# Four edits to the attention half of a bucketed-attention and mixture-of-experts kernel: PSUM banks of the turned halves, order of the routing work, copies between partition halves, making of the first heads

## The chip, the cores and the metric

One core of a Trainium2 chip runs the whole kernel. The metric is the device time in microseconds (us), the median of several runs, lower is better. Engines are named as the profile names them: PE (TensorE), DVE (VectorE), ACT (ScalarE), POOL (GpSimd), SP (SyncE, which here only issues DMAs).

## The reference

Attention over 4 batches, 8 heads, 768 positions, head size 64, in which a query sees only the keys that fall into its own hash bucket (6 sign bits of a projection); its result is fed to a top-1 mixture of 8 experts.

```python
q_bits = (einsum('bhsd,dk->bhsk', q, proj) > 0); k_bits = (einsum('bhsd,dk->bhsk', k, proj) > 0)
mask = q_bucket[:, :, :, None] == k_bucket[:, :, None, :]
scores = np.where(mask, q @ k.T / np.sqrt(D), -1e9)
attn = softmax(scores)                        # with 1e-9 added to the sum
x = (attn @ v)                                # (3072 tokens, 512)
e_idx = argmax(x @ w_gate); gate_w = softmax(x @ w_gate)[e_idx]
eom = sigmoid(x @ w_output_gate)
out[t] = gate_w * eom[e_idx] * (relu(x @ w1[e_idx]) @ w2[e_idx])
```

## The kernel before

**Heads and steps.** Heads are taken in 16 pairs. A pair is 12 steps, a step is 128 queries of one head; 192 steps, in blocks of 6 (`PER`). Each step has two parts that run 6 steps apart (`LAG`): `scores(s)` (L539) makes 8 matmuls into a `ps_s` tile, two `float32r` terms of queries against two of keys (`qh`, `ql`, `kh`, `kl`: high and low parts) and one product of bucket bits (`bb`); DVE reads the tile back into `sc` with its row minimum (L542); `soft` (L550) is the exponential on ACT; `normal` (L557 to L560) makes reciprocals of the row sums on DVE and scales `sc` on POOL; `transposed` (L580) turns `sc` on PE, 12 transposes of 64x64 blocks into two PSUM tiles (first and second half), which ACT copies to `pts` (L586). Once a block, `weighted` (L597) multiplies `pts` with `v`.

**PSUM.** `ps_s` and `ps_t` have two buffers each, `ps_a` and `ps_m` one. The first turned half always goes to `ps_t`. The second goes to `ps_t` at k = 0 (k is the step's place in its block), to `ps_m` at odd k, to `ps_a` at even k (L572 to L575). `weighted` accumulates in `ps_a`; the projection to bits (`project`, L436), `logits` (L631), `tokens` (L641), `prefix` (L698) and `table` (L239) use `ps_m`.

**Making a head.** For each head, POOL makes `qh`, `kh` (L488, L489), DVE makes `ql`, `kl` (L494, L497). Rows 0 to 63 of a tile hold the first half of the positions, 64 to 127 the second; both partition halves must hold all queries, so SP copies the halves across: four copies of `qh`, `ql` (L501, L502) and six of the bits (L517). The first head is made apart (`first_head`).

**Routing.** After each batch the tokens' experts, gates and table entries are worked out in small pieces (`routing`) that are planned into the steps of the next batch: `block(step, when, fn)` puts a piece at a named place inside the first step of a block ("early", "amid", "logits", "matmuls", "behind"), `plan(step, fn)` at a step's end. The order on PE, DVE, ACT and POOL is the order in which the program is written (`MANUAL`); SP's order is chosen by the scheduler.

**Late part and experts.** From step 170 on (`late`), the busiest expert's first weights are loaded and split on POOL (`early_w1`, L180 and L183) while attention ends. After the last step come the experts (L325), in which PE has almost no idle time; the change leaves them as they are.

Of the kernel before, what the change touches and what calls it, by code (L numbers as in the profile page):

```python
# [20 lines left out]
NB = 6  # L21
P = 128
# [37 lines left out]
def lsh_attention_then_moe(  # L60
# [22 lines left out]
    nc.scalar.dma_start(pj, proj)  # L83
    thr, scl, set0 = (pj[:, D + i:D + i + 1] for i in range(3))
    pjc = cst.tile([P, 2, 32], F32, name="pjc")
    nc.vector.memset(pjc, 0.0)

    def signed():

        for h in range(2):  # L90
            hs = slice(h * D, (h + 1) * D)
            src = pj[hs, 32 * h:32 * h + NB]
            for m, sg in ((0, 1.0), (1, -1.0)):
                c = 2 * NB * h
                nc.gpsimd.tensor_scalar(pjc[hs, m, c:c + NB], src, sg, 0.0, ALU.mult, ALU.add)
                nc.gpsimd.tensor_scalar(pjc[hs, m, c + NB:c + 2 * NB], src, -sg, 0.0, ALU.mult, ALU.add)
# [124 lines left out]
    def table_rhs(pool, oa, oh, gt, tk, n):  # L221

        rhs = pool.tile([P, 3, n, E * NCH], F32, name="t_rhs")
        nc.vector.tensor_tensor(rhs[:, 2].rearrange("p n (e a) -> p n e a", e=E),
                                oh[:, :, :, None].broadcast_to([P, n, E, NCH]),
                                oa[:, :, None, :].broadcast_to([P, n, E, NCH]), ALU.mult)
        for i, val in ((0, tk), (1, gt)):
            nc.vector.tensor_tensor(rhs[:, i], rhs[:, 2], val[:, :, None].broadcast_to([P, n, E * NCH]), ALU.mult)
        return rhs
# [155 lines left out]
    with ExitStack() as actx:  # L385
# [11 lines left out]
        at, around = {}, {}  # L397

# [26 lines left out]

        def bits_of(g, j):
            return halves[(2 * g + j) % 4]
# [15 lines left out]
        def tiles(g, j):  # L443
            st = pairs[g]
            for k, n in (("qh", S), ("ql", S), ("kh", HS), ("kl", HS)):
                st.setdefault(k, [None, None])[j] = hp.tile([P, n], F32R, name=k)
            return (st[k][j] for k in ("qk", "qh", "ql", "kh", "kl"))

        def first_head():

            qk, qh, ql, kh, kl = tiles(0, 0)
            bb = bits_of(0, 0)
            first = slice(0, HS)
            pp = ps_m.tile([P, HS], F32, name="ps_m")
            for m in range(2):
# [3 lines left out]
            nc.scalar.activation(qh[:, first], qk[:, first], AF.Copy, scale=-0.125)  # L459
            nc.vector.tensor_tensor(kl, qk[:, KEYS], f32(kh), ALU.subtract)  # L460
            nc.vector.scalar_tensor_tensor(ql[:, first], qk[:, first], -0.125, f32(qh[:, first]),
                                           ALU.mult, ALU.subtract)
            bt = hp.tile([P, HS], F32R, name="bt", bufs=2)
            nc.vector.tensor_scalar(bt, pp, 0.0, set0, ALU.is_gt, ALU.is_equal)
            bt = f32(bt)
            for h in range(2):
# [4 lines left out]
            def query_bits(n, h):  # L471
                c = (n ^ h) * HS
                nc.scalar.activation(bb[h * D:h * D + 2 * NB, c:c + HS], bt[32 * n:32 * n + 2 * NB], AF.Copy, scale=PEN)

            query_bits(0, 0)
            query_bits(0, 1)
            nc.vector.scalar_tensor_tensor(ql[DOWN, KEYS], qk[UP, first], -0.125, f32(qh[UP, first]),
                                           ALU.mult, ALU.subtract)
            for x in (qh, ql):
                nc.sync.dma_start(f32(x)[UP, KEYS], f32(x)[DOWN, first])  # L480
            return query_bits

        def split_hi(g, j):
            qk, qh, ql, kh, kl = tiles(g, j)
            if g == 0:
                nc.scalar.activation(qh[:, 0:HS], qk[:, 0:HS], AF.Copy, scale=-0.125)
            else:
                nc.gpsimd.tensor_scalar(qh[:, 0:HS], qk[:, 0:HS], -0.125, 0.0, ALU.mult, ALU.add)  # L488
            nc.gpsimd.tensor_scalar(kh, qk[:, KEYS], 1.0, 0.0, ALU.mult, ALU.add)  # L489

        def split_lo(g, j, m):
            st = pairs[g]
            if m == 0:
                nc.vector.scalar_tensor_tensor(st["ql"][j][:, 0:HS], st["qk"][j][:, 0:HS], -0.125,  # L494
                                               f32(st["qh"][j][:, 0:HS]), ALU.mult, ALU.subtract)
            else:
                nc.vector.tensor_tensor(st["kl"][j], st["qk"][j][:, KEYS], f32(st["kh"][j]), ALU.subtract)  # L497

        def turn_over(x):
            x = f32(x)  # L500
            nc.sync.dma_start(x[DOWN, KEYS], x[UP, 0:HS])  # L501
            nc.sync.dma_start(x[UP, KEYS], x[DOWN, 0:HS])  # L502

        def spread_hi(g, j):
            turn_over(pairs[g]["qh"][j])

        def spread_lo(g, j):
            turn_over(pairs[g]["ql"][j])

        def spread_bits(g, j):  # L510
            bt, bb = f32(pairs[g]["bt"]), f32(bits_of(g, j))
            for m in range(2):
# [32 lines left out]
        def soft(s, sc, mn):  # L545
            if s % GROUP == 0:
                sums[s // GROUP] = sp.tile([P, GROUP], F32, name="rsum")
# [3 lines left out]
                                 accum_out=sums[s // GROUP][:, k:k + 1])  # L551
# [10 lines left out]
        def transposed(s, pr):  # L562
# [10 lines left out]
            else:  # L573
                second = (ps_t, "ps_t") if last or s % PER == 0 else (ps_m, "ps_m") if s % 2 else (ps_a, "ps_a")
# [10 lines left out]
            for h in range(2):  # L585
# [33 lines left out]
        def routing(b):  # L619
# [112 lines left out]
            def columns():  # L732
                st["rhs"] = table_rhs(gp, st["oa"], oh, gate[:, ts], toki[:, ts], NT)
# [22 lines left out]
        for g in range(NP):  # L756
            s0 = 12 * (g - 1)
            if g >= 2:
                if g > 2:
                    plan(max(s0 - 20, 9), lambda g=g: load(g, (0,)))  # L760
                    plan(max(s0 - 16, 10), lambda g=g: load(g, (1,)))
                    block(s0 - PER, "matmuls", lambda g=g: project(g))
                else:
                    plan(10, lambda g=g: project(g))
                for j in range(2):
                    block(s0 + PER * j, "head", lambda g=g, j=j: split_hi(g, j))
                    block(s0 + PER * j, "early", lambda g=g, j=j: split_lo(g, j, 0))
                    block(s0 + PER * j, "amid", lambda g=g, j=j: split_lo(g, j, 1))
                    block(s0 + PER * j, "behind", lambda g=g, j=j: spread(g, j))
            elif g == 1:  # L770
                plan(1, lambda: split_hi(1, 0), lambda: spread_hi(1, 0))
                plan(2, lambda: project(1), lambda: split_hi(1, 1), lambda: spread_hi(1, 1))
                plan(3, lambda: load(2, (0,)))
                for j in range(2):
                    plan(3, lambda j=j: spread_bits(1, j))
                    for m in range(2):
                        plan(4 + 2 * j + m, lambda j=j, m=m: split_lo(1, j, m))
                    plan(5 + 2 * j, lambda j=j: spread_lo(1, j))
                plan(5, lambda: load(2, (1,)))
                plan(6, lambda: load_v(0))  # L780
            if g >= 1:
# [469 lines left out]
```

## Time and profile before

| | |
|---|---|
| median of 3 runs | 784.33 us (783.89 to 787.59) |
| profiled execution, its own time | 785.98 us |
| its span, first to last instruction | 784.3 us |
| PE busy | 731.6 us, 93% |
| mean granted TensorE clock | 0.971 of full speed |
| attention, to 2 us after the last step's scores are read (L542) | 457.8 us |
| from there to the end | 326.5 us |

The profile is one execution. The span leaves out 1.7 us around it. Matmuls are pipelined, so a busy PE is not PE at its peak, but a stretch in which PE has idle time or a granted clock below 1 has time that PE itself did not need. A block is cut in the tables where its first `sc` instruction (L542) starts.

### The profile page before, as it was taken

The numbers are of one execution on the slowest core, as the hardware profiler recorded it, in microseconds if no ns is written. First come the engines' busy times: TensorE is split into PE (matmuls) and PEld (weight loads), VectorE is DVE, ScalarE is ACT, GpSimd is POOL, SyncE is SP. The second block draws the span as 40 slices with busy tenths as digits, with TensorE's granted clock in tenths as the row PEclk, the third lists the DMA queues.
The fourth block names the chain that finished last, engine by engine and source line by source line (L and its number), as shares of the span: only waits on it lengthen the run. The fifth ranks groups of instructions, "written<-read, shape, count | busy, mean of one in ns | idle before, by whom it ended". The sixth has DMA issues, their size and how long they took to land. (4 is left out here: it accounts for less than half of the span.)

```text
span 784.3 us, 17592 instructions
## 1 busy us (share of the span) xinstructions
PE 731.6 (93%) x6591; PEld 602.3 (77%) x6591; DVE 493.6 (63%) x1046; ACT 452.3 (58%) x927; POOL 372.5 (47%) x446
## 2 busy tenths in 40 slices
PE   6699999988998988999798899999999999999996
PEld 4568776666875676775586568988999999989894
DVE  7578777768776866776788668236262636364640
ACT  4579888857787775887786751244251524353330
POOL 4355655444354534445347851552527273646201
PEclk9799999989999997999999999999999999999999
DMA  6344545324254333344325322374444444446501
GB/s 192 102 114 84 120 101 119 83 69 117 70 119 92 101 70 86 91 105 96 70 43 158 74 83 37 102 251 135 145 147 153 151 152 150 149 154 216 199 10 39
DMA packets 86878, 89.16 MB, mean 114 GB/s; under 512 B 58887, under 2 KB 69183, under 8 KB 86784
## 3 DMA queue, kind: packets, MB, share of 16 engines
q1 hardware_dynamic: 81440, 74.60, 35.5%
q0 software_dynamic: 5200, 13.31, 5.2%
q8 instruction: 54, 0.88, 0.5%
q14 instruction: 40, 0.33, 0.1%
q10 hardware_dynamic: 144, 0.03, 0.0%
HBM read 59.51 MB, written 13.11 MB: 93 GB/s over the span
## 5 line engine op out<-in xcount | busy, mean ns | idle before, releaser
L560 POOL TENSOR_SCALAR sc<-sc,rsum 128x768 f32<-128x768 f32 x192 | 180.3, 954 | 209.9 <-DVE rsum L558 101.5
L542 DVE TENSOR_SCALAR_CACHE_REDUCE sc<-ps_s 128x768 f32<-128x768 f32 x192 | 182.8, 954 | 66.7 <-PE ps_s L539 63.3
L550 ACT ACTIVATE sc<-sc,mn 128x768 f32<-128x768 f32 x192 | 179.1, 940 | 30.9 <-DVE sc L542 30.8
L586 ACT COPY pts<-ps_t 128x384 f32<-128x384 f32 x220 | 104.0, 488 | 86.3 <-PE ps_t L580 46.3
L597 PE MATMUL ps_a<-pts,vt 128*64 128x384 f32 x768 | 136.1, 490 | 0.0
L580 PEld LDWEIGHTS ps_t<-ident,sc 64*128 64x128 f32 x1338 | 98.7, 143 | 32.3 <-issue 17.4
L580 PE MATMUL ps_t<-ident,sc 64*128 64x64 f32 x1338 | 110.7, 231 | 3.1 <-ACT pts L586 3.1
L597 PEld LDWEIGHTS ps_a<-pts,vt 128*64 128x64 f32 x768 | 74.3, 137 | 50.7 <-issue 22.5
L336 DVE SCALAR_TENSOR_TENSOR hl<-ps_s,hh 128x256 fp32r<-128x256 f32 (+8 forms) x40 | 34.0, 849 | 105.7 <-ACT hh L335 79.8
L325 PE MATMUL ps_s<-xh,w1h 128*128 128x256 f32 (+7 forms) x288 | 97.0, 337 | 0.1
L325 PE MATMUL ps_s<-xlo,w1h 128*128 128x256 f32 (+7 forms) x288 | 95.4, 331 | 0.0
L325 PE MATMUL ps_s<-xh,w1l 128*128 128x256 f32 (+7 forms) x288 | 95.2, 330 | 0.0
L299 POOL DMA_INDIRECT xq<-x_dram,idx x75 | 82.2, 1096 | 23.8 <-issue 20.5
L539 PE MATMUL ps_s<-kh,qh 64*128 64x384 f32 x384 | 90.2, 444 | 2.5 <-DVE sc L542 2.5
L346 POOL DMA_INDIRECT out_dram<-yo,sid x29 | 31.1, 1073 | 119.1 <-ACT yo L343 68.1
L335 ACT ACTIVATE hh<-ps_s 128x256 fp32r<-128x256 f32 (+8 forms) x40 | 29.1, 727 | 96.4 <-PE ps_s L325 80.3
L539 PE MATMUL ps_s<-kh,ql 64*128 64x384 f32 x384 | 73.2, 351 | 2.1 <-DMA ql<-ql 2.1
L539 PE MATMUL ps_s<-bb 64*128 64x384 f32 x384 | 73.1, 350 | 0.2 <-POOL bb L468 0.2
L539 PE MATMUL ps_s<-kl,qh 64*128 64x384 f32 x384 | 72.6, 352 | 0.0
L580 PE MATMUL ps_m<-ident,sc 64*128 64x64 f32 x558 | 53.5, 232 | 9.5 <-DVE bt L440 7.1
L580 PEld LDWEIGHTS ps_m<-ident,sc 64*128 64x128 f32 x558 | 47.1, 144 | 12.8 <-DVE bt L440 7.8
L325 PEld LDWEIGHTS ps_s<-xh,w1h 128*128 128x128 f32 x288 | 54.2, 188 | 2.1 <-issue 0.6
(219 smaller groups left out, 1457.6 us busy)
## 6 DMA issues: line engine op xcount, KB each, us to landing
w_raw<-in_w_dram SPq DMA_DIRECT2D x34, 512.0 KB
qk<-in_qkT_dram SPq DMA_DIRECT2D x32, 384.0 KB
xh<-in_w_dram SPq DMA_DIRECT2D x14, 512.0 KB
xlo<-in_w_dram SPq DMA_DIRECT2D x14, 512.0 KB
vt<-in_v_dram SPq DMA_DIRECT2D x16, 384.0 KB
qh<-qh SPq DMA_DIRECT2D x63, 96.0 KB
ql<-ql SPq DMA_DIRECT2D x63, 96.0 KB
x_dram<-xb SPq DMA_DIRECT2D x60, 96.0 KB
```

Source lines behind the costliest of these rows:

```text
L299: nc.gpsimd.indirect_dma_start(out=xq[:, k * P:(k + 1) * P], out_offset=None, in_=x_dram.rearrange("n (a f) -> (n a) f", a=NB32), in_offse ...
L325: nc.tensor.matmul(ps, l, r, start=first and k == 0, stop=last and k == len(pairs) - 1)
L335: nc.scalar.activation(hh, ph, AF.Relu)
L336: return lambda: nc.vector.scalar_tensor_tensor(hl, ph, 0.0, f32(hh), ALU.max, ALU.subtract)
L346: nc.gpsimd.indirect_dma_start(out=out[:, :], out_offset=bass.IndirectOffsetOnAxis(ap=sid[0:n, r, a:a + 1], axis=0), in_=yo[0:n], in_offse ...
L539: nc.tensor.matmul(ss[:, h, 0:HS], q[rs, c:c + P], k[rs, 0:HS], start=(i == 0), stop=(i == 3))
L542: nc.vector.tensor_scalar(sc, ss[:, :, 0:HS], MASKED, None, ALU.min, ALU.min, accum_out=mn)
L550: nc.scalar.activation(pr, pr, AF.Exp, bias=mn, scale=-1.0, accum_out=sums[s // GROUP][:, k:k + 1])
L560: nc.gpsimd.tensor_scalar(live[s0 + k], live[s0 + k], rs[:, k:k + 1], 0.0, ALU.mult, ALU.add)
L580: nc.tensor.transpose(trs[h][:, c], pr[r, c * P:(c + 1) * P], ident[r, r])
L586: (nc.vector.tensor_copy if h and last else nc.scalar.copy)(pts[:, :, t * P + h * hq:t * P + (h + 1) * hq], trs[h])
L597: nc.tensor.matmul(st["av"][j * D:(j + 1) * D], st["v"][:, j, c], blocks[hb][j][:, c], start=(c == 0), stop=(c == NT - 1))
```

## The change

- **Banks.** Steps of the turned part at which `project`, `tokens`, `prefix`, `table` or their reads need `ps_m` are kept in a set `held`. The second half goes to `ps_t` at a held k = 0, to `ps_m` at an even k that is not held, to `ps_a` otherwise. The second half is copied out ahead of the first. PE's instructions stay 7390 in number; of the 64x64 transposes 654 go to `ps_a` (372 before) and 378 to `ps_m` (558 before).
- **Routing.** `prefix`, `table`, `entries` and other pieces are moved to other steps, `gate_sums` out of the block of `choose`, `t_rhs` to POOL for the first three batches; `xb`'s transposes come a block later, ahead of the reads of the split. The last exponential of a block moves from k = 1 to k = 2.
- **Copies.** `qh`, `ql` lie in one tile `qhl`, so that one copy moves a half of both; the bits are laid 5 partitions apart, so that one copy fills both partition halves: 6 copies a head for 10. SP's order is now the written one too. Loads of `qk` move some steps ahead.
- **GpSimd.** `kl` of 30 heads moves from DVE to POOL; `rsum` becomes a reduction over a pair (the sum and a preset 1e-9).
- **First heads.** Both heads of the first pair are made in one function; two of four zero fills move from DVE to POOL, and eight small POOL instructions for the projection become one, with a second small load.
- **Late part.** `early_w1` is split into halves over more steps, `early_gather` and `early_turn` come later.

```diff
+        FIRST, EVERY = 4, 5
+        terms = [cst.tile([P, GROUP, 2], F32, name="terms", bufs=4) for _ in range(4)]
...
-        def first_head():
+        def first_heads(t):
...
+            signed(t)
+            nc.gpsimd.tensor_scalar(kh1, qk1[:, KEYS], 1.0, 0.0, ALU.mult, ALU.add)
             nc.vector.tensor_tensor(kl, qk[:, KEYS], f32(kh), ALU.subtract)
...
+            nc.vector.tensor_tensor(kl1, qk1[:, KEYS], f32(kh1), ALU.subtract)
+            spread(0, 1)
...
+        def spread_half(g, j, h):
+            x = f32(pairs[g]["x"][j])
+            to, at = (DOWN, UP) if h else (UP, DOWN)
+            nc.sync.dma_start(x[to, :, KEYS], x[at, :, 0:HS])
+
+        def spread_bits(g, j, m):
+            bt, bb = f32(pairs[g]["bt"]), f32(bits_of(g, j))
+            rows = slice(FIRST, FIRST + 4 * NB * EVERY, EVERY)
+            r = 32 * (2 * j + m)
+            nc.sync.dma_start(bb[rows, m * S:m * S + HS], bt[r:r + 4 * NB])
+
+        def spread_bits_half(g, j, h):
...
         def spread(g, j):
+            spread_bits(g, j, 1)
+            spread_bits(g, j, 0)
+            for h in (1, 0):
+                spread_half(g, j, h)
+                spread_bits_half(g, j, h)
...
-            rs = sums.pop(s0 // GROUP)
-            nc.vector.tensor_scalar(rs, rs, 1e-9, None, ALU.add)
+            rs = sp.tile([P, GROUP], F32, name="rsum")
+            nc.vector.tensor_reduce(rs, sums.pop(s0 // GROUP), AX.X, ALU.add)
...
-                second = (ps_t, "ps_t") if last or s % PER == 0 else (ps_m, "ps_m") if s % 2 else (ps_a, "ps_a")
+                second = (ps_t, "ps_t") if last or s in held and s % PER == 0 else (
+                    ps_m, "ps_m") if s % 2 == 0 and s not in held else (ps_a, "ps_a")
...
-            for h in range(2):
+            for h in (1, 0):
                 (nc.vector.tensor_copy if h and last else nc.scalar.copy)(
...
                 for j in range(2):
-                    block(s0 + PER * j, "head", lambda g=g, j=j: split_hi(g, j))
-                    block(s0 + PER * j, "early", lambda g=g, j=j: split_lo(g, j, 0))
-                    block(s0 + PER * j, "amid", lambda g=g, j=j: split_lo(g, j, 1))
+                    n = s0 + PER * j
+                    plan(n - 1, lambda g=g, j=j: split_hi(g, j))
+                    block(n, "early", lambda g=g, j=j: split_lo(g, j, 0))
+                    plan(n + 3, lambda g=g, j=j: split_lo(g, j, 1, nc.gpsimd))
...
-            block(s0 + 3 * PER, "amid", r["choose"], r["gate_sums"])
-            block(s0 + 5 * PER, "amid", r["gate_values"], r["columns"])
+            block(s0 + 3 * PER, "amid", r["choose"])
...
+            plan(s0 + 34, r["columns"])
+            block(s0 + 6 * PER, "amid", r["hot"])
...
+            held.update(s0 + n - LAG for n in (8, 14, 20, 22, 38))
...
-            plan(late + 12 + 2 * a, lambda a=a: early_turn(a))
+            plan(late + 25 + 2 * a, lambda a=a: early_turn(a))
...
-        with tc.manual_schedule(engines=MANUAL):
+        with tc.manual_schedule(engines=MANUAL | {mybir.EngineType.SP}):
```

**SP, first steps.** Before, from the first copies on (`qk` are loads, `qh`, `ql`, `bb` the copies between halves):

```order
L501 DMA qh<-qh 64x384
L502 DMA qh<-qh 64x384
L517 DMA bb<-bt 12x384 x12
L501 DMA ql<-ql 64x384
L502 DMA ql<-ql 64x384
L415 DMA qk<-in_qkT_dram 128x768
```

After, from the start:

```order
L415 DMA qk<-in_qkT_dram 128x768 x4
L517 DMA bb<-bt 24x384 x2
L511 DMA qhl<-qhl 64x2x384
L523 DMA bb<-bt 12x384
L511 DMA qhl<-qhl 64x2x384
L523 DMA bb<-bt 12x384
L493 DMA qhl<-qhl 64x384 x2
L415 DMA qk<-in_qkT_dram 128x768 x2
```

The single `qk` of the first fence is the second load of the third pair; it stood behind 30 copies. Both loads of that pair, the `qk` x2 of the second fence, now stand behind 8.

**DVE, the block in which `choose` stands** (steps 66 to 71; `eq` to `ohb` are `choose`, `den`, `en`, `es` are `gate_sums`). Before:

```order
L494 SCALAR_TENSOR_TENSOR ql<-qk,qh 128x384
L497 TENSOR_TENSOR kl<-qk,kh 128x384
L667 TENSOR_SCALAR eq<-df 128x48
L668 TENSOR_TENSOR eq<-eq,expi 128x48
...
L674 CAST ohb<-oneh 128x48
L678 TENSOR_REDUCE den<-ex 128x6
L679 TENSOR_TENSOR en<-en,oneh 128x48
L681 TENSOR_REDUCE es<-en 128x6
...
L600 COPY ot<-ps_a 128x384
L440 TENSOR_SCALAR bt<-ps_m,pj 128x384
L609 STREAM_TRANSPOSE xb<-ot 128x384
L542 TENSOR_SCALAR sc,mn<-ps_s 128x768 x2
```

After:

```order
L618 STREAM_TRANSPOSE xb<-ot 128x384
L503 SCALAR_TENSOR_TENSOR qhl<-qk,qhl 128x384
L676 TENSOR_SCALAR eq<-df 128x48
L677 TENSOR_TENSOR eq<-eq,expi 128x48
...
L683 CAST ohb<-oneh 128x48
L565 TENSOR_REDUCE rsum<-terms 128x2
L566 RECIPROCAL rsum<-rsum 128x2
L609 COPY ot<-ps_a 128x384
L443 TENSOR_SCALAR bt<-ps_m,pj 128x384
L550 TENSOR_SCALAR sc,mn<-ps_s 128x768 x3
```

`kl` and `gate_sums` are gone from between the block's start and the read of `ps_m` (`bt`), and `xb` no longer stands between `bt` and the next `sc`.

**ACT, the same block** (`sc` are exponentials, `pts` the copies out of the turned halves). Before:

```order
L550 ACTIVATE sc,rsum<-sc,mn 128x768 x5
L586 COPY pts_2781<-ps_t 128x6x64 x2
L550 ACTIVATE sc,rsum<-sc,mn 128x768
L586 COPY pts_2782<-ps_t 128x6x64
L586 COPY pts_2782<-ps_m 128x6x64
L586 COPY pts_2781<-ps_t 128x6x64
L586 COPY pts_2781<-ps_a 128x6x64
```

After:

```order
L558 ACTIVATE sc,terms<-sc,mn 128x768 x5
L595 COPY pts_2711<-ps_t 128x6x64 x2
L595 COPY pts_2712<-ps_a 128x6x64
L595 COPY pts_2712<-ps_t 128x6x64
L595 COPY pts_2711<-ps_a 128x6x64
L595 COPY pts_2711<-ps_t 128x6x64
L558 ACTIVATE sc,terms<-sc,mn 128x768
```

The second halves of k = 1 and k = 2 both go to `ps_a`, `ps_m` stays with the routing, and the sixth exponential stands behind four more copies.

## Rows read from the trace of the kernel before

**Rows 1.** Page, busy time, share and instructions of each engine.
```profile
PE 731.6 (93%) x6591; PEld 602.3 (77%) x6591; DVE 493.6 (63%) x1046; ACT 452.3 (58%) x927; POOL 372.5 (47%) x446
```
**Rows 2.** Stretches: length, busy PE, PEld, DVE, ACT, POOL, clock, DMA share, GB/s.
```profile
0.00:39.29 39.29, 26.98 (x221) 18.75 (x223) 24.32 (x51) 18.85 (x39) 15.95 (x31) 0.87 0.49 146
39.29:398.19 358.90, 333.42 (x3962) 253.08 (x3960) 267.70 (x666) 272.98 (x635) 175.12 (x239) 0.96 0.41 94
398.19:457.76 59.57, 52.27 (x604) 39.95 (x602) 44.34 (x110) 43.81 (x102) 39.81 (x36) 0.97 0.39 98
457.76:784.30 326.54, 318.88 (x1810) 290.57 (x1810) 157.29 (x220) 116.70 (x155) 141.59 (x140) 1.00 0.41 135
316.34:327.58 11.24, 11.24 (x145) 8.89 (x144) 8.82 (x21) 10.23 (x25) 4.72 (x6) 1.00 0.35 87
327.58:340.45 12.87, 12.51 (x153) 9.40 (x152) 10.19 (x25) 10.48 (x25) 8.42 (x10) 1.00 0.52 117
151.45:170.93 19.48, 15.61 (x161) 12.10 (x161) 13.34 (x40) 10.83 (x26) 8.46 (x10) 0.82 0.37 83
```
**Rows 3.** Waits of PE, whole span: us in total, times, longest us.
```profile
PE ps_m L698 <- ACT pts L586: 7.7, 3, 2.6
PE ps_m L580 <- DVE bt L440: 7.1, 5, 1.7
PE ps_m L641 <- ACT pts L586: 6.5, 7, 1.7
PE ps_m L436 <- DMA qk<-in_qkT_dram: 4.8, 1, 4.8
PE ps_m L239 <- ACT pts L586: 2.7, 3, 0.9
PE ps_s L539 <- DMA ql<-ql: 2.1, 1, 2.1
```
**Rows 4.** Timeline of SP's queue, first steps: start, us, instruction, count.
```profile
19.35 9.51 SPq L517 DMA_DIRECT2D bb<-bt  x12
...
30.23 0.55 SPq L415 DMA_DIRECT2D qk<-in_qkT_dram  x1
```
**Rows 5.** Timeline of PE: the projection at step 10, `prefix` at step 67.
```profile
34.24 1.49 PE L436 MATMUL ps_m<-qk,pjc 128*32 128x384 f32 x4 [4.76 <-DMA qk<-in_qkT_dram]
...
162.25 0.20 PE L698 MATMUL ps_m<-ohb,tri 128*128 128x48 bf16 x1 [2.56 <-ACT pts L586]
```
**Rows 6.** Timelines of POOL, DVE and ACT around `choose` and `prefix`.
```profile
153.36 3.87 POOL L560 TENSOR_SCALAR sc<-sc,rsum 128x768 f32<-128x768 f32 x4 [7.42 <-ACT sc L550]
...
154.81 0.71 DVE L668 TENSOR_TENSOR eq<-eq,expi 128x48 f32<-128x48 f32 x1
...
159.46 0.92 DVE L542 TENSOR_SCALAR_CACHE_REDUCE sc<-ps_s 128x768 f32<-128x768 f32 x1
...
160.43 0.94 ACT L550 ACTIVATE sc<-sc,mn 128x768 f32<-128x768 f32 x1 [2.64 <-DVE sc L542]
```
**Rows 7.** Groups by line, steps' part: busy us, mean ns, idle before and releaser.
```profile
L497 DVE TENSOR_TENSOR kl<-qk,kh 128x384 fp32r<-128x384 f32 x31 | 23.0, 743 | 0.9 <-POOL kh L489 0.9
...
L560 POOL TENSOR_SCALAR sc<-sc,rsum 128x768 f32<-128x768 f32 x192 | 180.3, 954 | 209.9 <-DVE rsum L558 101.5 <-ACT sc L550 68.9 <-ACT pts L586 22.7
...
L183 POOL TENSOR_TENSOR w1l<-w_raw,w1h 128x1024 fp32r<-128x1024 f32 x4 | 9.4, 2361 | 0.3
L180 POOL TENSOR_SCALAR w1h<-w_raw 128x1024 fp32r<-128x1024 f32 x4 | 4.9, 1230 | 0.0
```
**Rows 8.** Single lines: count, shortest, median and longest ns, first and last start.
```profile
L517 SPq DMA_DIRECT2D bb<-bt x186: 713/765/1894, 10.7 to 408.3; - x186
...
L668 DVE TENSOR_TENSOR eq<-eq,expi x4: 210/712/712, 154.8 to 475.4; 128x48 f32<-128x48 f32 x4
```

More of the change, by code (lines that the diff above doesn't have):

```diff
@@ L397, in lsh_attention_then_moe @@
         at, around = {}, {}
+        held = set()
         LAG = PER
@@ L444, in tiles @@
             st = pairs[g]
-            for k, n in (("qh", S), ("ql", S), ("kh", HS), ("kl", HS)):
-                st.setdefault(k, [None, None])[j] = hp.tile([P, n], F32R, name=k)
+            x = hp.tile([P, 2, S], F32R, name="qhl")
+            st.setdefault("x", [None, None])[j] = x
+            for k, t in (("qh", x[:, 0]), ("ql", x[:, 1]), ("kh", None), ("kl", None)):
+                st.setdefault(k, [None, None])[j] = hp.tile([P, HS], F32R, name=k) if t is None else t
             return (st[k][j] for k in ("qk", "qh", "ql", "kh", "kl"))
-        def first_head():
+        def first_heads(t):
             qk, qh, ql, kh, kl = tiles(0, 0)
+            qk1, qh1, ql1, kh1, kl1 = tiles(0, 1)
             bb = bits_of(0, 0)
@@ L465, in first_head @@
             bt = f32(bt)
+            nc.vector.scalar_tensor_tensor(ql[:, first], qk[:, first], -0.125, f32(qh[:, first]),
+                                           ALU.mult, ALU.subtract)
             for h in range(2):
@@ L469, in first_head @@
                                         ALU.mult, ALU.add)
[L471 to L476, printed above, removed]
+            project(0, ps_a.tile([P, HS], F32, name="ps_a"), (1,))
+            for n in range(2):
+                for h in range(2):
+                    c = (n ^ h) * HS
+                    nc.scalar.activation(bb[h * D:h * D + 2 * NB, c:c + HS], bt[32 * n:32 * n + 2 * NB],
+                                         AF.Copy, scale=PEN)
@@ L546, in soft @@
             if s % GROUP == 0:
-                sums[s // GROUP] = sp.tile([P, GROUP], F32, name="rsum")
+                sums[s // GROUP] = terms[s // GROUP % len(terms)]
             pr = sc.rearrange("p a b -> p (a b)")
@@ L786, in lsh_attention_then_moe @@
                 if g + 1 < NP:
-                    plan(12 * g + 6 * hf + 2 * PER, lambda g=g, hf=hf: rows(g, hf))
+                    block(12 * g + 6 * hf + 3 * PER, "early", lambda g=g, hf=hf: rows(g, hf))
         for i, fn in enumerate(more_constants()):
@@ L919, in lsh_attention_then_moe @@
             turn_idle(12)
-            query_bits = first_head()
-            split_hi(0, 1)
-            spread_hi(0, 1)
-            project(0, ps_a.tile([P, HS], F32, name="ps_a"), (1,))
-            split_lo(0, 1, 1)
-            split_lo(0, 1, 0)
-            spread_bits(0, 1)
-            spread_lo(0, 1)
-            query_bits(1, 0)
-            query_bits(1, 1)
+            first_heads(t)
             turn_idle(1)
@@ L932, in lsh_attention_then_moe @@
             raw = []
-            few = [s for s in range(2 * PER, NSTEP, PER) if s % (2 * PER) == 0 or s // PER == 2 * NP - 3]
+            few = []
             def softs(n):
@@ L966, in lsh_attention_then_moe @@
                 elif k == 0:
-                    now("head")
                     softs(2)
```

168 lines of the change are left out of this document (83 added, 85 removed).

## The prediction, made before the changed kernel was run

> **What bounds the kernel now.** I read the page's busy times first: PE is busy for 93% of the span, no other engine for more than 63% [rows 1]. So the end is set by PE, and two things can shorten the time: PE's idle time, and stretches in which PE ran below full speed. Next I cut the span into stretches [rows 2]. From 457.76 on (the experts) PE is busy nearly throughout at a clock of 1.00, and the change touches nothing there. Before that, in 457.76 us, PE is idle for 12.31 us at the start (39.29 less 26.98), 25.48 in the middle and 7.30 in the late blocks: 45.1 us. The granted clock is 0.87, 0.96 and 0.97 in these three. It has two levels, 1.2 and 2.4 GHz, so a mean of 0.87 says that 26% of the stretch ran at the lower; at full speed the same columns would have taken 13% less. That is 0.13 x 39.29 + 0.04 x 358.90 + 0.03 x 59.57 = 5.1 + 14.4 + 1.8 = 21.3 us at most. If everything were won, 785.98 (the profiled execution's own time) would fall to 719.6.
>
> Undisturbed blocks show the floor. An even block lasts 11.24 us with PE busy throughout; an odd one, with a projection, 12.87 with 0.36 idle; both at 1.00. ACT is next at 10.2 to 10.5, so there is no second engine to run into until a block is cut below that. The block with `choose` and `prefix` takes 19.48 us: 3.87 idle and a clock of 0.82 [rows 2]. The lower clock comes in blocks with the long stalls, none is in the clean ones.
>
> PE's list of waits says where the idle time ends [rows 3]. `prefix`, `tokens` and `table` wait for ACT to copy a turned half out of `ps_m`, the single bank that they share with it: 7.7 + 6.5 + 2.7 us. Turned halves wait for DVE to read the projection (`bt`) out of the same bank: 7.1. Together 24.0. Two waits are for DMAs, 4.8 and 2.1, both at the start.
>
> **The change part by part.**
>
> *Banks and routing, in the middle stretch.* PE's work stays as it is, 7390 instructions; only banks and places differ. At each step at which routing or a projection wants `ps_m`, the turned half now goes elsewhere, so the 24.0 us have no cause left, apart from the share in the late blocks, which I put at 4 of the 7.3 idle there: 20 us here. What is behind them is shown by `prefix` [rows 5, 6]: PE stood 2.56 us until a copy by ACT; ACT had stood 2.64 us for DVE's `sc`, which started only at 159.46, because `choose`, `gate_sums`, `kl`, `bt` and `xb` stood ahead of it. The new order takes `kl`, `gate_sums` and `xb` from there, so the second link is loosened too. The lower clock follows these stalls, so I take its 14.4 us as gone with them. Sum 34 us. The ends: 14 if a wait for `ps_a` takes over (first rival) and 39.9 if the small waits for `ps_t` go as well. I take 34, near the upper end, since each bank's reader is named in the order and had time to finish.
>
> *First heads and copies.* The second part of the projection at step 10 waited 4.76 us for a load that SP issued at 30.23, behind 12 copies that alone took from 19.35 to 28.86 [rows 4, 5]. Now it stands behind 8 copies, and is issued some 10 us before it is needed. The 2.1 us for `ql` [rows 3] go as well if six copies do what ten did. The copy of 12 rows took 0.765 us [rows 8]. One of 24 rows is not in the trace: between 0.765 and 1.53. Bits of a head then cost 2 x 0.765 + 2 x (0.765 to 1.53) = 3.1 to 4.6 us on SP where they cost 6 x 0.765 = 4.6; a copy of both `qh` and `ql` carries the bytes of two, and costs at most the two. So SP never gets slower, and all heads' copies are covered as they were, by a block of 11 us. Of 12.31 + 5.1 = 17.4 us in the start I take 13: 4.8 + 2.1 by name, the lower clock (5.1) which follows them, and 1 of the rest. Ends: 4.8 (the load alone) and 17.4.
>
> *GpSimd.* `kl` of 30 heads leaves DVE: 30 x 0.743 = 22 us less there [rows 7], off the path in clean blocks (DVE 8.8 to 10.2 of 11.2 to 12.9). POOL gets it at 2.361 x 384/1024 = 0.89 us each, an estimate from its own subtraction of 1024 columns, 27 us in all. A clean odd block then has POOL at 8.42 + 0.89 = 9.3 of 12.87: covered; without that cover it would be 0.89 a block. `t_rhs` on POOL, three times, is bounded by zero and one `sc` scaling (0.954) an instruction, 9 instructions: at most 2.9 us in each of three blocks, where 12.87 - 9.3 = 3.6 are left. Counted at zero. `rsum`'s reduction replaces an instruction one for one: zero.
>
> *Late blocks.* 7.3 idle + 1.8 clock. Splitting the weights is the same work, 4 x (2.361 + 1.230) = 14.4 us on POOL [rows 7], in eight pieces instead of four and nearer to the end. Ends: 9.1 gained, or 3 lost if the last piece makes the first expert wait. I take 4, the middle of the range.
>
> Sum: 34 + 13 + 4 = 51 us, 785.98 - 51 = 735. The median of the runs is 1.65 below the profiled execution, so I forecast **733 us**. Its own range is 719 to 748, from the ends.
>
> **The rivals.**
>
> *A wait for `ps_a` takes the place of the one for `ps_m`.* `ps_a` gets 654 transposes for 372, up to three steps in succession with one bank, while `weighted` wants it too. The sixth exponential (0.94 us) stands between two copies, so a step can find the bank full. For it: PE has waited for ACT's copies before [rows 3]. Against: the second half is now copied first, and a step's scores give ACT time. The middle then gives 14 instead of 34: 733 + 20 = 753 us.
>
> *The bank is only where it shows.* If DVE's lateness sets the stall (ACT waited 2.64 us for `sc` before PE waited 2.56 for ACT [rows 5, 6]), freeing banks moves the wait to `ps_s`, and only start and late part gain: 785.98 - 17 - 1.65 = 767 us. Against: three of the things ahead of `sc` have left.
>
> *POOL holds DVE up.* `eq` on DVE took 0.21 us at its shortest and 0.71 at its longest [rows 8], the latter while POOL scaled `sc` [rows 6]. If each `kl` on POOL delays a DVE instruction that PE waits for by its full length, that is 30 x 0.89 = 27 us: 760 us. Against: DVE has 1 to 2 us free in a clean block. The Trainium skill, "SBUF — State Buffer", section "Who interferes with whom", states the rule: DVE and GpSimd share one pair of ports as an exclusive lock, which a DVE instruction with two SBUF inputs wants when GpSimd reads SBUF, so a longer GpSimd instruction blocks it longer. The trace agrees in the 0.71 us of `eq`, whose two inputs lie in SBUF; it speaks against moving `kl`.
>
> *Copies come late: slower.* SP's order is now the written one, so a load that must wait for its tile (the next pair's `qk` waits for `kl`, now on POOL three steps into the block) holds up the copies behind it. In the written order it stands ahead of the copies of the second head of each pair, 15 of the 30. If those land late by x, PE loses 15 x, and from x = 3.4 us on that eats the 51. The load issued at 30.23 was used at 34.24, 4.0 us later [rows 4, 5]: with x = 4.0 the loss is 60 us, and the time 733 + 60 = 793 us, 9 above the time before. Against: in the clean blocks SP's queue kept pace with 8 more copies a pair, and a head has a block of 11 us for its copies.
>
> **How the numbers follow.** Forecast 0.60; `ps_a` 0.15; DVE's lateness 0.12; POOL 0.08; late copies 0.05. About 0.5%, 4 us, is what a measurement of this kernel can tell from no change. All but the last end below 780: faster 0.93, no change 0.02 (the last rival with x near its point of balance), slower 0.05. For 8 in 10 the range goes from 718 (719.6 less 1.65, everything won) to 764, which takes in the `ps_a` and POOL rivals and leaves out DVE's lateness and late copies.
>
> **What would show it.** Right: PE's waits for `ps_m` under 5 us in all; the clock at 1.00 in the middle; a `choose` block near 13 us; the scores' last step at about 407 us instead of 457; the stretch of the experts still 326. Wrong: waits of PE for `ps_a` by ACT in every block (first rival), for `ps_s` by DVE in the routing blocks (second), DVE's short instructions at 0.7 us and more outside `choose` (third), PE waiting for `qhl` or `bb` by DMA (fourth).

## The result, and the profile after

The changed kernel takes **728.66 us** (median of 4 runs, 726.28 to 729.74) where the one before took 785.11: a ratio of 0.9273, 95% interval 0.9238 to 0.9309. The forecast of 733 with its range of 718 to 764 holds. The profiled execution took 729.64, with a span of 727.8 us.

The page's busy times now read so, against [rows 1]:

```profile
PE 713.2 (98%) x6591; PEld 584.1 (80%) x6591; DVE 462.6 (64%) x1008; ACT 456.1 (63%) x927; POOL 398.5 (55%) x489
```

PE is idle for 14.6 us of the whole span. The stretches that answer to [rows 2] (in that order: start, middle, late blocks, the rest; then a clean even block, a clean odd one, the block with `choose`; columns as there):

```profile
0.00:28.24 28.24, 25.10 (x221) 17.64 (x223) 22.93 (x51) 18.32 (x39) 15.68 (x26) 1.00 0.58 169
28.24:346.54 318.30, 317.22 (x3968) 236.16 (x3968) 243.21 (x632) 277.28 (x637) 198.70 (x274) 1.00 0.46 107
346.54:396.29 49.75, 48.17 (x597) 36.33 (x594) 38.69 (x107) 42.27 (x98) 38.80 (x46) 1.00 0.40 99
396.29:727.84 331.55, 322.70 (x1815) 293.95 (x1810) 157.79 (x222) 118.20 (x157) 145.32 (x146) 0.98 0.43 137
295.73:306.90 11.17, 11.17 (x148) 8.73 (x150) 8.42 (x21) 10.46 (x26) 7.28 (x10) 1.00 0.59 119
283.64:295.73 12.09, 12.09 (x153) 9.06 (x152) 8.76 (x23) 10.46 (x26) 6.81 (x9) 1.00 0.41 103
134.85:148.82 13.97, 13.97 (x168) 10.12 (x168) 12.30 (x34) 11.81 (x28) 8.83 (x12) 1.00 0.32 90
```

The start is 11.05 us shorter, the middle 40.6, the late blocks 9.8; the rest is 5.0 longer. Together that is 56.5 us, the fall of the span from 784.3 to 727.8. In the middle PE is idle for 1.1 us instead of 25.5, and the half clock is gone. The block with `choose` falls from 19.48 to 13.97. A clean odd block falls from 12.87 to 12.09, which is more than the 0.36 us that it stood idle. PE's longest waits, against [rows 3]:

```profile
PE ps_a L589 <- DVE ot L609: 1.9, 4, 1.1
PE ps_t L589 <- POOL sc L568: 1.6, 1, 1.6
PE ps_t L945 <- POOL ident masks.py:199: 1.4, 1, 1.4
...
PE ps_m L589 <- DVE tacc_e L241: 0.7, 3, 0.2
```

The waits for `ps_m`, 24.0 us before, are down to 0.7 for turned halves. In the middle all of this reads as forecast. Attention ends at 396.3, ahead of the forecast 407, and the rest, which was to stay at 326, takes 331.5. The experiments show that the reason given for the middle was half of it.

### The profile page after: what moved, and what is told of

It reads as the page before. It is cut to its first block, busy times and chain, and to the rows that moved or that the text cites. A ratio compares the mean times of both kernels' runs of the same rounds, so it can differ in the third digit from the quotient of the medians.

```text
span 727.8 us, 17398 instructions
## 1 busy us (share of the span) xinstructions
PE 713.2 (98%) x6591; PEld 584.1 (80%) x6591; DVE 462.6 (64%) x1008; ACT 456.1 (63%) x927; POOL 398.5 (55%) x489
## 5 line engine op out<-in xcount | busy, mean ns | idle before, releaser
L568 POOL TENSOR_SCALAR sc<-sc,rsum 128x768 f32<-128x768 f32 x192 | 173.2, 916 | 137.3 <-PE ps_a L589 76.8
L547 PE MATMUL ps_s<-kh,qhl 64*128 64x384 f32 x768 | 152.2, 379 | 0.6 <-DVE sc L550 0.6
L606 PEld LDWEIGHTS ps_a<-pts,vt 128*64 128x64 f32 x768 | 68.6, 137 | 57.6 <-issue 13.9
L595 ACT COPY pts<-ps_t 128x384 f32<-128x384 f32 x203 | 98.0, 490 | 14.8 <-PE ps_t L589 14.8
L589 PE MATMUL ps_t<-ident,sc 64*128 64x64 f32 x1236 | 104.6, 226 | 2.3 <-POOL sc L568 1.6
L334 ACT ACTIVATE hh<-ps_s 128x256 fp32r<-128x256 f32 (+8 forms) x40 | 29.1, 726 | 99.0 <-PE ps_s L324 71.8
L547 PEld LDWEIGHTS ps_s<-kh,qhl 64*128 64x128 f32 x768 | 81.1, 190 | 4.8 <-DVE sc L550 1.7
L547 PE MATMUL ps_s<-kl,qhl 64*128 64x384 f32 x384 | 68.4, 335 | 0.0
L595 ACT COPY pts<-ps_a 128x384 f32<-128x384 f32 x109 | 52.3, 480 | 24.9 <-PE ps_a L589 21.4
L589 PE MATMUL ps_a<-ident,sc 64*128 64x64 f32 x654 | 59.3, 224 | 1.9 <-DVE ot L609 1.9
L589 PEld LDWEIGHTS ps_a<-ident,sc 64*128 64x128 f32 x654 | 54.2, 138 | 4.4 <-DVE ot L609 2.9
```

What stands on the lines that cost most here:

```text
L334: nc.scalar.activation(hh, ph, AF.Relu)
L547: nc.tensor.matmul(ss[:, h, 0:HS], q[rs, c:c + P], k[rs, 0:HS], start=(i == 0), stop=(i == 3))
L568: nc.gpsimd.tensor_scalar(live[s0 + k], live[s0 + k], rs[:, k:k + 1], 0.0, ALU.mult, ALU.add)
L589: nc.tensor.transpose(trs[h][:, c], pr[r, c * P:(c + 1) * P], ident[r, r])
L595: (nc.vector.tensor_copy if h and last else nc.scalar.copy)(pts[:, :, t * P + h * hq:t * P + (h + 1) * hq], trs[h])
L606: nc.tensor.matmul(st["av"][j * D:(j + 1) * D], st["v"][:, j, c], blocks[hb][j][:, c], start=(c == 0), stop=(c == NT - 1))
```

## The experiments

Times below are medians, each with its ratio to the kernel before, measured beside it. A stretch is the same piece of the program in every kernel (to block 2, to block 28, to the last scores, to the end), read from the profiled execution.

**The banks alone** (the kernel before with the new rule, the held steps and the order of copies):

```diff
- second = (ps_t, "ps_t") if last or s % PER == 0 else (ps_m, "ps_m") if s % 2 else (ps_a, "ps_a")
+ second = (ps_t, "ps_t") if last or s in held and s % PER == 0 else (
+     ps_m, "ps_m") if s % 2 == 0 and s not in held else (ps_a, "ps_a")
...
- for h in range(2):
+ for h in (1, 0):
...
+ held.update(s0 + n - LAG for n in (8, 14, 20, 34))
```

> The kernel before with the bank rule alone: second halves go to ps_a or ps_m by the new rule, steps around the old places of project, tokens, prefix and table are held, the second half is copied first. Routing, copies, kl and first heads stay as before. Theory (the shared bank is the cause): the 24.0 us of waits for ps_m mostly go, and the lower clock in the middle with them, so 785 falls by 20 to 35 us, to 750 to 765; the start stays at 39 us. Rival (DVE's lateness is the cause, the bank only where it shows): the waits move to ps_s or to DVE's sc, and the gain is under 10 us, 775 to 785.

Measured: 763.28, ratio 0.9735 [0.9715, 0.9755], so 21 us. The head of its list of PE's waits, then the timeline of one wait for `ps_t` with the copy by ACT ahead of it:

```profile
PE ps_a L582 <- ACT pts L588: 11.5, 12, 1.5
PE ps_t L582 <- issue: 5.7, 8, 0.9
PE ps_a L582 <- DVE ot L602: 5.6, 6, 1.8
```

```profile
214.38 0.48 ACT L588 COPY pts<-ps_t 128x384 f32<-128x384 f32 x1
214.96 0.24 PE L582 MATMUL ps_t<-ident,sc 64*128 64x64 f32 x1 [0.66 <-issue]
```

The waits for turned halves and for copies in `ps_m` are gone, and `ps_a` stands in their place, released by the same copies of ACT: the first rival, as the prediction described it. For the eight waits for `ps_t` ("issue") the profile names no releaser, but each of them ends 0.10 us after a copy of ACT out of `ps_t` has ended, as here (214.86, 214.96). The middle shrinks by 18.3, not 34, and mostly by its clock:

```profile
38.85:379.46 340.61, 321.09 (x3962) 235.03 (x3962) 267.06 (x666) 274.25 (x635) 174.95 (x239) 1.00 0.43 99
```

The half clock is gone from it, but PE is still idle for 19.5 us where it was 25.5.

**The banks undone** (the change with the old rule and order of copies):

```diff
- second = (ps_t, "ps_t") if last or s in held and s % PER == 0 else (
-     ps_m, "ps_m") if s % 2 == 0 and s not in held else (ps_a, "ps_a")
+ second = (ps_t, "ps_t") if last or s % PER == 0 else (ps_m, "ps_m") if s % 2 else (ps_a, "ps_a")
...
- for h in (1, 0):
+ for h in range(2):
```

> The changed kernel with the bank rule and the order of the two copies as they were before, all else as changed. Theory (bank): PE's waits for ps_m by ACT and DVE come back at the steps of project, tokens, prefix and table; 729 rises by 10 to 30 us, to 739 to 759. Rival (DVE's lateness): since the routing is spread out, almost nothing comes back, 729 to 735.

Measured: 735.57, 0.9386 [0.9368, 0.9404]: only 7 us are lost, less than the theory's 10 and just above the rival's 735. PE again waits for `ps_m`, now mostly by DVE:

```profile
PE ps_m L588 <- DVE tot L718: 4.3, 3, 1.4
PE ps_m L588 <- DVE tacc_e L241: 4.1, 3, 1.4
```

So most of the middle's gain stands without the freed banks. Something else in the change carries it.

**The exponential ahead of the copies.** The diff has an edit that the prediction gave no term: `few` is emptied, and the sixth exponential of every block stands at step 2, after the copies of the turned halves. Before, odd blocks (all but one) had it at step 1, ahead of the copies; even blocks had it at step 2 already, and their fifth at step 1. The same edit moves `normal` of the block's last two steps (DVE's `rsum`, POOL's scaling of `sc`) to step 4; before it stood at step 2 in odd blocks and in the next block in even ones. This run puts the sixth exponential at step 1 in every block of the change, with `normal` at step 2:

```diff
- elif k == 4:
+ elif k == 1:
+     normals()
+     softs(1)
+ elif k == 2:
      normals()
...
- if k == 2 and s > 2 * PER or s - 1 in few or PER < s < 2 * PER and k in (1, 2, 4):
+ if s - 1 in few or PER < s < 2 * PER and k in (1, 2, 4):
```

> The changed kernel with the last exponential of a block at k = 1 ahead of the copies, as the odd blocks had it before, all else as changed. The odd blocks of the middle fell from 12.87 to 12.1 us, more than their 0.36 us of idle time. Theory (the sixth exponential stood between two copies and PE waited for it): odd blocks go back to 12.5 to 12.9, 13 of them, and even blocks grow too, by 0.3 or more; 729 rises by 5 to 15 us. Rival (the 0.7 us come from banks or from kl): within 4 us.

Measured: 759.67, 0.9685 [0.9659, 0.971]: 31 us lost, twice the theory's upper end, with PE waiting 17.5 us for `ps_a` by ACT's copies and 11.6 more for `ps_t` (each of these 18 waits again ends 0.10 us after ACT's copy). The blocks come to 12.15 and 12.91 us.

**The exponentials exactly as before**, in the change (even blocks at step 2, odd ones at step 1):

```diff
- few = []
+ few = [s for s in range(2 * PER, NSTEP, PER) if s % (2 * PER) == 0 or s // PER == 2 * NP - 3]
...
- elif k == 4:
+ elif k == 1:
+     normals()
+     softs(1)
+ elif k == 2:
...
- if k == 2 and s > 2 * PER or s - 1 in few or PER < s < 2 * PER and k in (1, 2, 4):
+ if s - 2 in few or PER < s < 2 * PER and k in (1, 2, 4):
```

> The change with the exponentials exactly as before (even blocks: the fifth at step 1, the sixth at step 2; odd blocks: the sixth at step 1, ahead of the copies). The run with every block's sixth exponential at step 1 took 759.67, with 0.8 us more in each odd block and 0.95 in each even one. Theory "the exponential's place": only the odd blocks pay, 14 times 0.8 and up to 4 more in the routed blocks, 740 to 746, PE waiting for ps_a <- ACT pts about 9 us. Rival "the banks carry it": 728 to 733.

Measured: 747.96, 0.953 [0.9514, 0.9546]: 19 us lost, 2 more than the theory's upper end, and far from the rival's 733. Its waits:

```profile
PE ps_a L589 <- ACT pts L595: 11.4, 13, 1.4
PE ps_t L589 <- issue: 5.0, 8, 0.7
```

The timelines show the link (start, us, instruction, idle before it). In the clean odd block of the kernel before (lines of ACT, PE and DVE in order of time):

```profile
333.02 0.86 ACT L586 COPY pts<-ps_t 128x384 f32<-128x384 f32 x2 [0.88 <-PE ps_t L580]
...
334.01 0.22 PE L580 MATMUL ps_m<-ident,sc 64*128 64x64 f32 x1
...
334.90 0.94 ACT L550 ACTIVATE sc<-sc,mn 128x768 f32<-128x768 f32 x1 [1.02 <-DVE sc L542]
...
335.84 0.46 ACT L586 COPY pts<-ps_t 128x384 f32<-128x384 f32 x1
...
336.02 0.16 DVE L557 TENSOR_SCALAR rsum<-rsum 128x2 f32<-128x2 f32 x1
...
336.44 0.24 PE L580 MATMUL ps_t<-ident,sc 64*128 64x64 f32 x1 [0.31 <-ACT pts L586]
```

and at the same place in the change:

```profile
289.13 0.86 ACT L595 COPY pts<-ps_t 128x384 f32<-128x384 f32 x2 [0.90 <-PE ps_t L589]
290.39 0.48 ACT L595 COPY pts<-ps_a 128x384 f32<-128x384 f32 x1 [0.39 <-PE ps_a L589]
...
292.26 0.95 ACT L558 ACTIVATE sc<-sc,mn 128x768 f32<-128x768 f32 x1
```

Before, ACT came to the exponential first and stood 1.02 us for DVE's `sc`, while turned halves that were ready (the last of their transposes started at 334.01) waited behind it on ACT's queue: from the start of that pair of copies to the next copy it took 2.8 us, and PE's transposes two steps on waited for that copy. Now the next copy starts 1.3 us after the pair does, and the exponential, four copies later, waits for nothing. `normal`, moved by the same edit, is not what PE waited for here: `rsum` on DVE waited for nothing at 336.02, and PE's wait ended with ACT's copy. No run moves the two apart, so in the blocks with routing the share of `normal` stays open. Over the span the exponentials wait for `sc` for 5.3 us where it was 30.8 (the page's groups, of before and of after):

```profile
L550 ACT ACTIVATE sc<-sc,mn 128x768 f32<-128x768 f32 x192 | 179.1, 940 | 30.9 <-DVE sc L542 30.8
```

```profile
L558 ACT ACTIVATE sc<-sc,mn 128x768 f32<-128x768 f32 x192 | 178.4, 937 | 5.3 <-DVE sc L550 5.3
```

**The exponential alone, and with the banks.** Both start from the kernel before; the first has this edit alone, the second has it on top of the banks:

```diff
- few = [s for s in range(2 * PER, NSTEP, PER) if s % (2 * PER) == 0 or s // PER == 2 * NP - 3]
+ few = []
...
- elif k == 1:
-     normals()
-     softs(1)
- elif k == 2:
+ elif k == 4:
      normals()
...
- if s - 2 in few or PER < s < 2 * PER and k in (1, 2, 4):
+ if k == 2 and s > 2 * PER or PER < s < 2 * PER and k in (1, 2, 4):
```

> The kernel before with one edit: the sixth exponential of every block at its step 2, behind the step's copies, and the normal work at step 4, as in the change; banks, routing, copies and start stay. In the kernel before the odd blocks alone have it at step 1 (12.88 us against 11.24 of the even ones). Theory "the exponential's place carries most of the middle": the odd blocks come to about 12.1 and the choose and table blocks lose some of their half clock, 758 to 768 in all. Rival "the banks carry the middle, and the exponential's place counts only once they are free": 778 to 786, with ps_m still the longest of PE's waits. If neither is enough alone (two conditions in series): 770 to 778.

> The kernel before with the banks, the held steps and the order of copies (763.28 alone) and the exponential's place as well; routing, spread copies, kl and start stay as before. If these two edits are the whole of the middle's 40.6 us: 785 - 41 = 744, with part of the late blocks' 9.8 on top 738 to 746; odd blocks at 12.1, choose block at about 14. If the routing's spreading is needed too: 750 to 758, choose block over 15. If the banks were all: 760 to 764.

Measured: the exponential alone 755.9, 0.9618 [0.9601, 0.9634], 29 us and so more than the banks alone, and 2 more than the theory's best end. Both together: 735.86, 0.9369 [0.9354, 0.9385], 49 us, again 2 below the range, since the late blocks gained 8.0 as well. The stretches of both together, to be read against those of the change:

```profile
0.00:38.75 38.75, 28.20 (x220) 17.92 (x221) 24.32 (x52) 18.32 (x39) 15.55 (x31) 0.87 0.50 148
38.75:356.66 317.91, 317.16 (x3969) 235.02 (x3968) 260.92 (x667) 277.07 (x637) 171.09 (x238) 1.00 0.45 105
356.66:408.23 51.57, 49.78 (x605) 37.47 (x603) 41.69 (x110) 43.43 (x100) 38.98 (x38) 1.00 0.45 110
408.23:733.60 325.37, 318.14 (x1804) 290.39 (x1800) 157.54 (x220) 116.30 (x154) 140.69 (x141) 1.00 0.41 136
```

The middle is 317.9 against the change's 318.3: two edits are the whole of it. The exponential alone leaves 10.1 us of idle time in the middle, and in it the stalls of `choose` and `table`, each with a clock of 0.90 (the middle, then its first two blocks of that kind, 17.26 and 17.75 us):

```profile
39.71:374.57 334.86, 324.72 (x3969) 245.63 (x3969) 262.81 (x667) 277.11 (x637) 171.65 (x238) 0.98 0.43 100
147.27:164.53 17.26, 15.72 (x169) 11.80 (x169) 13.10 (x40) 12.11 (x27) 8.01 (x11) 0.90 0.43 98
174.37:192.12 17.75, 15.56 (x165) 12.23 (x164) 12.65 (x33) 10.57 (x25) 7.42 (x10) 0.90 0.41 94
```

**Routing at the old steps** (the change, with `choose` and `gate_sums` together again and `t_rhs` on DVE):

```diff
...
- block(s0 + 3 * PER, "amid", r["choose"])
...
+ block(s0 + 3 * PER, "amid", r["choose"], r["gate_sums"])
+ block(s0 + 5 * PER, "amid", r["gate_values"], r["columns"])
...
+ (s0 + 15, r["best"]), (s0 + 19, r["prefix"]), (s0 + 20, r["offsets"]),
```

> The changed kernel with the routing of the first three batches at its old steps (gate_sums in the block of choose, prefix at step 19, table at 33, t_rhs on DVE), held steps set accordingly; banks, copies, kl and first heads as changed. Theory (bank): most of the gain stays, 729 to 740. Rival (DVE's lateness): the choose blocks grow again from 14.0 towards 19 us and the blocks with t_rhs from 12.1 towards 18, 3 x 10 us in all, 750 to 760.

Measured: 724.68, 0.9246 [0.9229, 0.9263], 4 us *less* than the change and below both expectations. The middle is 316.40 instead of 318.30, and the `choose` block stays at 13.9, so DVE's routing work in that block is not what sets the time. Where one of the other two edits is missing, the rest of the change still pays in the middle: with the old banks it is 334.9 without and 326.5 with it; with the old exponentials 340.6 and 335.6; with both edits made 317.9 and 318.3. These pairs differ in the routing, but also in `kl`, `rsum` and the copies, so it is not shown that the routing is what pays there.

**`kl` back on DVE, ten copies, SP's order left to the scheduler** (three runs, each the change with one of these):

```diff
- plan(n + 3, lambda g=g, j=j: split_lo(g, j, 1, nc.gpsimd))
+ plan(n + 3, lambda g=g, j=j: split_lo(g, j, 1))
```

> The changed kernel with kl of the 30 heads on DVE again, at the same step. Theory: kl lies beside other work on either engine, 729 within 4 us. Rival (POOL holds DVE up): with kl off POOL the short DVE instructions get faster and the time falls by 5 us or more. Other rival (DVE needs the room): time rises by 5 us or more, with PE waiting for ps_s.

```diff
- nc.sync.dma_start(x[to, :, KEYS], x[at, :, 0:HS])
+ for i in range(2):
+     nc.sync.dma_start(x[to, i, KEYS], x[at, i, 0:HS])
```

> The changed kernel with ten copies a head: the copies of both qh and ql and of both partition halves of the bits are each split in two; order, tiles and spacing stay. Theory (copies are covered by a block of 11 us): within 4 us of 729 in the middle, and the start longer by 1 to 4 us, since 4 more copies of 0.7 us stand ahead of the second head's use and of the third pair's load. Rival (SP's queue is near its limit): PE waits for qhl or bb by DMA in most blocks and the time rises by 10 us or more.

```diff
- with tc.manual_schedule(engines=MANUAL | {mybir.EngineType.SP}):
+ with tc.manual_schedule(engines=MANUAL):
```

> The changed kernel with SP's order left to the scheduler as before. Theory: only the start can change, by -1 to +8 us, if a load falls behind copies again; the middle stays. Rival (written order holds copies up): faster by 2 us or more.

Measured: 728.92, 0.9299 [0.9282, 0.9315]; 731.25, 0.9318 [0.9285, 0.9351]; 726.95, 0.9267 [0.9242, 0.9292]. All three intervals overlap that of the change. The first is no change in time. With ten copies, 2.6 more, the profiled execution loses time at one place: block 2 takes 15.8 us instead of 11.1, where PE waits 3.4 for the first load of `vt`, which SP issues at 25.72 instead of 23.22, and the clock falls to one half for 3.4 us. The third has the middle of the change to 0.1 us (318.41); on its start, 2.0 shorter, see the last section.

**The weights split earlier.** In the change the rest grows by 5.0 us. At 402.74 PE waits once for POOL, and behind that wait the clock is 0.50 (PE's timeline, then the stretch):

```profile
402.74 0.90 PE L589 MATMUL ps_t<-ident,sc 64*128 64x64 f32 x12 [1.57 <-POOL sc L568]
```

```profile
402.80:409.60 6.80, 6.80 (x64) 5.89 (x65) 3.60 (x6) 3.14 (x5) 6.66 (x7) 0.50 0.67 234
```

POOL's queue shows what it did instead: pieces of `w1` stand between the last scalings of `sc`, for which the last transposes wait.

```profile
398.05 1.79 POOL L568 TENSOR_SCALAR sc<-sc,rsum 128x768 f32<-128x768 f32 x2
399.81 0.63 POOL L917 TENSOR_SCALAR w1h<-w_raw 128x512 fp32r<-128x512 f32 x1
400.52 1.28 POOL L918 TENSOR_TENSOR w1l<-w_raw,w1h 128x512 fp32r<-128x512 f32 x1
401.77 1.79 POOL L568 TENSOR_SCALAR sc<-sc,rsum 128x768 f32<-128x768 f32 x2
```

So the pieces were put earlier, and their loads with them:

```diff
- plan(late + (0, 1, 15, 18)[cc], lambda cc=cc: early_load(cc))
+ plan(late + (0, 1, 11, 15)[cc], lambda cc=cc: early_load(cc))
...
- plan(late + 12 + (1, 2, 3, 5)[(2 * cc + h) % 4] + PER * (cc // 2), lambda cc=cc, h=h: early_w1(cc, h))
+ plan(late + (7, 9, 11, 13, 14, 15, 19, 20)[2 * cc + h], lambda cc=cc, h=h: early_w1(cc, h))
```

> The changed kernel with the eight pieces of the split of the first expert's weights on POOL 4 to 6 steps earlier (steps 175 to 188 for 181 to 191), and two of the loads 3 to 4 steps earlier. Theory (POOL's last pieces make PE wait 1.57 us for a scaled sc, and the clock falls for 6.8 us behind that): the stretch from the last scores to the first expert matmul falls from 11.3 to 7 to 9 us, 729 falls by 2 to 5. Rival (POOL then holds up earlier blocks as much): within 2 us, with PE waiting for POOL's sc in blocks 29 and 30.

Measured: 724.66, 0.9242 [0.9218, 0.9266], 4.0 less than the change. That wait and the half clock are gone, and the rest takes 327.7 instead of 331.5.

**Three edits together**: the old routing steps, the earlier splits and SP's order by the scheduler.

> The change with three edits that each brought something alone: routing at the old steps (-4.0), w1's pieces split earlier (-4.0), SP's order left to the scheduler (-1.7). If they are separate: 728.7 - 9.7 = 719. If the first two cure the same thing (POOL late for the last blocks, the wait of 1.6 us and the half clock behind it at 402.8 to 409.6): 721 to 724. If the earlier splits collide with the routing's work on POOL: 725 or more.

Measured: **722.45**, 0.9196 [0.9181, 0.9211], faster than both kernels; all its runs (721.91 to 722.70) lie below all of the change's. It is the middle case: the gains do not add up. With the routing at its old steps the rest was already 3.4 shorter, and its half clock there lasted 3.4 us instead of 6.8; how much of this is the routing's doing is not shown, since behind this wait the clock differed between kernels (last section). Its stretches are the last row here, beside those of the others, in us:

| kernel | start | middle | late | rest | span |
|---|---|---|---|---|---|
| before | 39.3 | 358.9 | 59.6 | 326.5 | 784.3 |
| banks alone | 38.9 | 340.6 | 57.8 | 324.5 | 761.8 |
| exponential alone | 39.7 | 334.9 | 54.6 | 326.6 | 755.8 |
| banks and exponential | 38.8 | 317.9 | 51.6 | 325.4 | 733.6 |
| the change | 28.2 | 318.3 | 49.8 | 331.5 | 727.8 |
| the change, banks undone | 29.1 | 326.5 | 50.3 | 327.8 | 733.7 |
| the change, exponentials as before | 26.0 | 335.6 | 52.9 | 329.9 | 744.5 |
| three edits | 27.3 | 316.6 | 49.4 | 327.5 | 720.8 |

## Why the prediction was right, and where its reason was not

**The sum** was 51 where 56.5 came. The likeliest case came true as a time, and PE's idle time and half clock were the right place to look. That the largest term came out near is luck: another edit of the same diff did the larger half of its work. The prediction's "own range" of 719 to 748 does not follow from its ends, which add up to 718 and 769; the late blocks' 4 is above the middle of their range, which is 3.

**Banks and routing, 34 us.** The middle gave 40.6, but this is the step that failed: "the 24.0 us have no cause left". With the banks alone PE waits 17.2 us for `ps_a` and `ps_t` behind ACT's copies instead, and 18.3 are won. The prediction walked through the diff and gave the exponential's new place no term; it named the sixth exponential only as what speaks for the first rival. It is the larger half: 24.0 alone (358.9 less 334.9), 41.0 with the banks. The two nearly add up (18.3 + 24.0 = 42.3), since they loosen two links: which bank a half may use, and when ACT empties it. Nor did the lower clock simply follow idle time: the banks alone took the half clock out of the middle and left 19.5 us of idle time there. The first rival's mechanism is real; the change avoids it by this edit, not because "a step's scores give ACT time". Routing, which the sum counted with the banks, adds nothing to the two. The upper end of 39.9 was passed too: it counted idle time and half clock, and a clean odd block lost 0.78 with 0.36 idle. All of this stands at the transposes that waited for ACT: from the start of those of one step to the start of those two steps on it is 3.06 us before (334.79 to 337.85) and 2.24 after (290.92 to 293.16). The stall is longer than the idle time that the profile books for it.

**First heads and copies, 13 us.** 11.05 in the profiled execution. The wait of 4.76 and the half clock went as said; DVE's first read of scores began hardly earlier (11.36 against 11.64). With ten copies, and with SP's order by the scheduler, the start is as short (27.6 and 26.3), so neither the count of copies nor the written order carries this term; the load's new place and the making of the first heads were not tried apart. Copies of 24 rows lie at the lower of the two ends. The fourth rival is out: SP in the written order and in the scheduler's gives the same middle, and for a spread copy PE's weight loads wait once, for 0.6 us.

**GpSimd, zero.** Right as a time, with a price of 1.01 us for `kl` instead of the estimated 0.89; DVE had 2.4 to 2.7 us free in a clean block, not "1 to 2". With `kl` on DVE the middle is 3.2 us longer (321.5) and the rest 3.0 shorter, which cancels. The rest is shorter there with no half clock at its start, though PE's wait was the same 1.56 us (last section). If that is chance, `kl` on POOL is worth some 3 us in the middle; no run's time shows it. The third rival is out: the time did not rise, and `eq` on DVE took 0.21 us in all four of its runs, where at least two of the four had taken 0.71 [rows 8]:

```profile
L677 DVE TENSOR_TENSOR eq<-eq,expi x4: 207/207/209, 137.7 to 418.5; 128x48 f32<-128x48 f32 x4
```

The rule of the Trainium skill ("SBUF — State Buffer", "Who interferes with whom") is not refuted by this: no scaling by POOL is under way any more when `eq` starts, and in three of the four runs one starts 0.07 us behind it. It only had no price in the time here.

**Late blocks, 4 us, and the experts, "still 326".** The late blocks gave 9.8, over the upper end of 9.1, and the banks and the exponential alone give 8.0 of it, with the weights split as before; but the rest lost 5.0 of it. The end "3 lost if the last piece makes the first expert wait" was the right danger in another place: the pieces hold up POOL's last scalings of `sc`, PE waits 1.6 us, and the half clock follows into the expert's stretch. Together 4.8, close to the 4 by two errors that cancel.

**The second rival** (DVE's lateness, 767) was nearer than it looked. ACT did wait for DVE's `sc`; what counted was that ACT's ready copies stood behind that wait. Moving the exponential behind them was enough; with DVE's routing work back at its old place the time was no worse.

## What to carry to other kernels

When a wait names a buffer, follow it to the engine that empties the buffer, and read that engine's own queue in order: an instruction that waits there for something else, ahead of one that is ready, is the cause as much as the buffer is. Give every edit of a diff a term, a moved line most of all, since a change of place has no instruction count to remind one of it. And where a stretch is said to be untouched, look at what the engines that feed it do last.

## What the runs showed of the hardware that was not expected

**A copy of 24 rows costs SP no more than one of 12.** In the change (shortest, median, longest ns), L517 copies 24 rows with a step of five rows, L523 copies 12:

```profile
L517 SPq DMA_DIRECT2D bb<-bt x62: 717/752/1937, 8.5 to 358.8; - x62
```

```profile
L523 SPq DMA_DIRECT2D bb<-bt x62: 745/751/782, 11.0 to 363.0; - x62
```

**PE's first matmuls come at different paces, while the clock reads 1.00.** The four of the first head's second projection took 1.50 us in the profiled execution of the change and 0.84 in that of the change with the exponentials as before, whose first heads are the same; between 4.6 us and DVE's first read of scores the clock's row reads 1.00 in both. That read began at 11.36 and at 9.74.

```profile
6.19 1.50 PE L439 MATMUL ps_a<-qk,pjc 128*32 128x384 f32 x4
```

```profile
5.97 0.84 PE L439 MATMUL ps_a<-qk,pjc 128*32 128x384 f32 x4 [0.45 <-POOL pjc L95]
```

Of the ten kernels with these first heads four had 1.50, five 0.84, and the one with ten copies 1.06. So up to 1.6 us of a start can differ between executions with the same work; why the pace differs is not shown. The profiled execution with SP's order by the scheduler had the quick pace, and its first read of scores began 1.5 earlier, at 9.86; whether its median, 1.7 less, has the same cause is not shown. The one with the earlier splits had the quick pace too, and a start 2.1 shorter than the change's.

**The same wait brings the half clock in some executions only.** PE waited 1.56 to 1.58 us for POOL's `sc` near the first expert in five kernels (the change, and it with `kl` on DVE, ten copies, the scheduler's SP order, the old routing steps). After it the clock was 0.50 for 6.8 us in two of them, for 3.4 in one, and stayed at 1.00 in two.
